# A new written order for a linear-attention and MLP block on one core: the memset behind the first statistics, thirteen warming products, keys and states regrouped

## The chip, the cores and the metric

The kernel runs on one core of one Trainium2 chip. The core has five engines that work side by side: TensorE (PE, with its weight loads as PEld) for matrix products, VectorE (DVE), ScalarE (ACT), GpSimd (POOL), and SyncE (SP), which here issues all transfers. The metric is the device time of one execution in microseconds (us), of which the median of several runs is given; a profiled execution gives the span of the trace, which is a little shorter than the device time.

## The reference

```python
def _A_ref(x, wqkv, wo):            # x: 1 x 2048 x 512, H = 32 heads of 16
    qkv = (x @ wqkv) split into q, k, v by head
    phi = lambda t: jnp.where(t > 0, t + 1, jnp.exp(t)) + 1e-6
    pq, pk = phi(q), phi(k)
    kv = jnp.einsum("bhsd,bhse->bhde", pk, v)
    z = jnp.einsum("bhsd->bhd", pk)
    num = jnp.einsum("bhqd,bhde->bhqe", pq, kv)
    den = jnp.einsum("bhqd,bhd->bhq", pq, z)[..., None] + 1e-6
    return (num / den) as 2048 x 512 @ wo

h = x + _A_ref(_layernorm(x), wqkv, wo)
h2 = h + relu(_layernorm(h) @ w1) @ w2      # w1: 512 x 1792, w2: 1792 x 512
```

All inputs and the output are bf16.

## The kernel before

The 2048 rows are 16 tiles of 128 (the first index of most steps), in four chunks of four tiles; 512 columns are four blocks of 128. The whole program is one table of words, `ORDER`. A word names a step and its indices: `K.3.7` is the key product of tile 3 into PSUM bank 7. A loop at the end of the kernel calls the steps in the table's order, with no scheduler behind it. So each engine runs its own steps exactly in the order of the words, and waits (by semaphores that are put in from the data) where an operand is not there yet. Moving a word moves instructions only against those of the same engine.

The steps that matter here:

- `lx`, `lk`, `lq`, `lv`, `lo`, `l1`, `l2` (L201, L204): loads of x, of the key, query and value parts of wqkv, of wo, w1 and w2, issued by SP. `const` (L174 to L178): four memsets on VectorE, the first of them of `zeros` (a row of `m_sb`), and the identity on POOL. `warm.n.b` (L215): n products 128x128 by 128x512 of `zeros` into bank b, whose result nobody reads.
- Layernorm of x: `S.t` statistics (L226, VectorE), `A.t` their aggregation (L227), `R.t.n` the reciprocal standard deviation of n tiles (L232 and L233, two activations on ScalarE), `N.t` the normalized tile (L251, VectorE). `T.t.b` transposes tiles 0 to 3 on TensorE (L270, four products by the identity), `E.t` copies the result out of PSUM (L280, ScalarE). Tiles 4 to 15 are transposed by DMA instead: `X.t` (L291), issued by SP.
- Keys: `K.t.b` (L299, four products of 128x512; `K.t.b.k.n` only n of them, from block k), then exp `F` (L317) and relu `U` (L320) on ScalarE, min `M` (L324) and sum `D` (L327) on VectorE, or `W` (L332) in place of `U` and `D`. The state x^T phi(k) is summed over the tiles by `G.t` (L351, four products) in banks 4 to 7. `Q` (L307) with `qF`, `qU`, `qM`, `qD`, `qW` are the same for queries. `za`, `zf`, `z` sum phi(k).
- `kv` (L392) multiplies the state by the value weights; `m` (L404) multiplies by wo; `dn` to `dm` make the denominator and scale the queries; `h` (L494) and `hD` (L500) are the attention's output plus x; `s`, `a`, `r`, `n` and `x` or `t`, `e` its layernorm and transposes.
- MLP: `p.c.f.b` (L510, four products), evacuated with relu in pairs by `pA` (L516, ScalarE) or `pD` (L521, VectorE); `f` (L530) the second product; `fo` (L538) scales and adds, `fd` (L545) stores.

There are eight PSUM banks, and the table names the bank of each product, so a product also waits until what its bank held is read.

Of the kernel before, what the change touches and what calls it, by code (L numbers as in the profile page):

```python
# [15 lines left out]


ORDER = """
const masks table lx.0.1 lx.1.1 lx.2.2 lk.0.2 lk.2.2 lx.4.2 lx.6.2 lx.8.4 lx.12.4 S.0 S.1 A.0 S.2 warm.1.6 A.1
R.0.1 S.3 A.2 R.1.1 warm.9.6 N.0 A.3 N.1 R.2.1 R.3.1 N.2 N.3 warm.1.6 T.0.2 T.1.7 T.2.5 S.4 E.0 S.5 T.3.4 A.4  # L20
K.0.3.0.2 E.1 K.1.0.0.2 E.2 E.3 A.5 R.4.2 K.0.3.2.2 S.7 F.0.1 N.5 S.6 K.3.7 M.0.1 K.2.2.0.2 U.0.1 A.7 A.6
K.1.0.2.2 D.0.1 F.3.1 U.3.1 R.6.2 N.4 K.2.2.2.2 M.3.1 G.0 D.3.1 G.3 F.2.1 F.1.1 N.6 N.7 S.8 S.9 X.5 X.4 M.2.1
A.8 A.9 U.2.1 U.1.1 K.5.1 R.8.2 K.4.0 M.1.1 D.2.1 F.4.2 D.1.1 N.9 U.4.2 N.8 X.7 S.12 X.6 X.9 G.2 K.7.3 S.13 A.12
A.13 G.1 K.6.2 K.9.1 M.4.2 S.10 R.12.2 F.6.2 N.12 D.4.2 S.11 A.10 U.6.2 X.8 lq.0.2 M.6.2 N.13 G.4 X.12 K.8.0
A.11 R.10.2 D.6.2 lv.0.2 X.13 G.5 G.6 N.10 N.11 S.15 S.14 F.8.2 M.8.2 U.8.2 G.7 X.11 A.15 A.14 D.8.2 R.14.2 N.15
K.12.0 N.14 za.2 za.4 X.10 G.9 lq.2.2 lv.2.2 K.13.1 K.11.3 F.12.2 U.12.2 X.15 X.14 l2.10.4 l2.3.4 l1.0.2 K.10.2
G.8 M.12.2 F.10.2 U.10.2 za.6 D.12.2 M.10.2 za.8 D.10.2 Q.0.0.0 Q.0.1.1 qF.0.0.2 qU.0.0.2 za.10 qM.0.0.2 K.15.3
G.12 K.14.2 F.14.2 G.11 Q.0.2.0 Q.0.3.1 qF.0.2.2 G.13 za.12 M.14.2 W.14.2 zf.12 qD.0.0.2 qM.0.2.2 qU.0.2.2 G.10
G.14 z.3.3.14 G.15 z.1.3.14 z.2.3.14 z.0.3.14 qD.0.2.2 zc Q.1.0.2 gA.0.2 gA.2.2 zh dn.0.1 Q.1.1.3 dnl.0 kv.0.4
kv.2.4 kv.1.4 kv.3.4 lo.0.2 lo.2.2 dnx.0.2.2 qF.1.0.2 dnx.0.0.2 Q.1.2.0 rt.2.7 kx qM.1.0.2 Q.1.3.1 qF.1.2.2  # L30
m.0.4 m.1.5 rv.2 qW.1.0.2 qM.1.2.2 Q.3.1.7 m.3.6 Q.2.3.2 l1.2.2 dt.3 mA.0.2 qW.1.2.2 dt.0 dt.1 m.2.5 Q.2.1.4
dn.1.3 mA.2.2 dm.0.0.2 dm.0.2.2 dnl.1 dnx.1.2.2 Q.2.2.1 h.3.6 dnx.1.0.2 h.1.5 hD.3 dt.7 qF.2.2.2 rt.6.3 s.3 dt.4
re.6 h.0.0 hD.1 qU.2.2.2 dt.5 a.3 hD.0 s.1 s.0 qM.2.2.2 a.0 Q.3.0.6 h.2.5 Q.2.0.3 n.3 n.0 a.1 dm.1.0.2 Q.3.2.0
Q.3.3.1 dm.1.2.2 x.0 x.3 hD.2 n.1 s.2 qF.3.0.2 qU.2.0.2 qF.2.0.2 h.5.2 h.6.3 a.2 qU.3.0.2 qF.3.2.2 qM.2.0.2
h.4.7 n.2 qD.2.0.2 t.2.5 qD.2.2.2 hD.5 hD.4 h.7.4 dn.2.6 hD.7 e.2 dnl.2 x.1 hD.6 qM.3.0.2 p.0.0.5 dnx.2.2.2
p.0.13.7 p.0.1.6 p.0.8.2 p.0.11.4 qD.3.0.2 s.4 dnx.2.0.2 p.0.9.3 l2.7.3 dt.10 pA.0.0.2 dt.11 l2.0.3 dt.9 dt.8
p.0.12.6 qM.3.2.2 qW.3.2.2 s.6 pD.0.12.2 p.0.3.1 p.0.2.0 pA.0.8.2 s.7 r.0.4 dn.3.6 p.0.5.3 p.0.4.2 a.7 dm.2.0.2
dnl.3 pA.0.2.2 dnx.3.0.2 dnx.3.2.2 pA.0.4.2 dm.2.2.2 p.0.7.7 h.9.0 h.8.5 p.0.6.6 n.7 s.5 dt.13 dt.12 p.0.10.3
hD.9 hD.8 s.8 a.6 pD.0.6.2 dt.15 a.4 n.6 dt.14 pA.0.10.2 f.1.1.0.7 dm.3.0.2 dm.3.2.2 h.11.0 f.1.1.7.7 h.12.4
fo.1 s.9 h.15.6 h.14.5 h.10.3 f.0.2.0.7 a.8 a.9 a.5 hD.11 n.5 hD.12 x.6 hD.15 f.3.4.0.7 h.13.7 f.3.4.7.7 x.7  # L40
s.12 n.8 n.4 hD.14 f.0.2.7.7 x.4 x.5 p.1.0.6 f.2.5.0.7 s.11 s.14 hD.13 fo.3 fo.0 hD.10 a.11 s.10 n.9 p.1.5.3
p.1.1.7 s.15 a.12 pA.1.0.2 p.1.4.2 f.2.5.7.7 p.1.13.7 p.1.3.1 a.10 n.12 r.4.4 pA.1.4.2 p.1.2.0 n.11 p.1.8.4 fo.2
a.14 a.15 s.13 p.1.12.6 n.10 p.1.7.2 pD.1.2.2 n.14 p.1.6.1 x.11 p.1.9.5 pA.1.6.2 x.10 a.13 n.15 x.9 x.8 pD.1.8.2
fd.3 f.5.3.0.7 f.7.0.0.7 p.1.10.1 fd.1 fd.0 pA.1.12.2 p.1.11.2 pA.1.10.2 p.2.9.7 p.2.11.6 f.7.0.7.7 p.2.10.5
p.2.5.1 f.5.3.7.7 fo.7 pD.2.10.2 p.2.8.6 p.2.4.0 r.8.4 f.4.4.0.7 f.4.4.7.7 fo.5 p.2.0.2 pD.2.8.2 pD.2.4.2
p.2.1.3 x.12 n.13 p.2.3.6 p.2.2.5 fd.2 f.6.0.0.7 x.14 x.13 pA.2.0.2 pA.2.2.2 x.15 fo.4 p.3.3.7 p.3.7.1 p.3.2.6
p.3.9.5 p.3.8.4 f.6.0.7.7 pD.3.2.2 fo.6 pD.3.8.2 fd.4 p.3.11.7 p.3.4.2 p.3.10.6 p.3.5.3 p.3.6.0 pA.3.10.2 fd.7
pA.3.6.2 p.2.7.7 fd.5 fd.6 p.2.6.6 pA.2.6.2 p.3.13.5 pD.3.4.2 p.3.0.1 p.3.1.2 p.2.13.7 p.2.12.6 f.11.3.0.7
p.3.12.4 pA.3.0.2 pA.2.12.2 r.12.4 pD.3.12.2 f.9.6.0.7 f.14.2.0.7 f.10.7.0.7 f.11.3.7.7 f.10.7.7.7 f.9.6.7.7
f.8.1.0.7 f.12.5.0.7 f.8.1.7.7 f.13.0.0.7 f.15.4.0.14.3.1 f.14.2.7.7 fo.9 fo.10 fo.11 fd.10 fd.11 fd.9  # L50
f.12.5.7.7 fo.8 f.13.0.7.7 f.15.3.0.14.0.2 fd.8 fo.14 fo.12 fo.13 fo.15.3.1 fd.12 f.15.1.0.14.2.1 fd.13
fd.15.3.1 fd.14 fo.15.0.2 fd.15.0.2 fo.15.2.1 fd.15.2.1
"""


# [525 lines left out]
```

## Time and profile before

| | |
|---|---|
| runs | 170.03, 170.32 and 171.63 us; median 170.32 |
| profiled execution | 170.08 us; span in the trace 168.4 us, TensorE's granted clock 0.999 in the mean |
| TensorE busy | 162.7 us, 97% of the span |
| VectorE busy | 101.2 us, 60% |
| ScalarE busy | 67.7 us, 40% |
| first warming product, first transpose, first key product | 1.25, 6.79 and 8.16 us |
| x tile 0 read by the first statistics | from 2.99 us |

Times are us from the start of the span. A row of the timeline has start, duration, engine, line, operation, written and read tiles, and in brackets the idle time ahead of it and what ended it; rows that follow each other closely are merged, with their count. A product shows 0.38 us from its start to its end but overlaps the next, so the distance of starts is what counts. The chain of work that ended last lists what each step was released by, so its pieces add up to the span.

### The profile page before, as it was taken

What the parts mean: (1) busy time and instruction counts of PE and PEld (TensorE: products, weight loads), DVE (VectorE), ACT (ScalarE), POOL (GpSimd) and SP (SyncE); (2) the same over time, 40 slices, a digit from 0 to 9 for tenths busy, and PEclk for the clock granted to TensorE, in tenths of its full rate; (3) what the DMA queues carried; (4) which work ended last, traced back from release to release, by engine and by line L of the source; (5) the groups of instructions that cost most, each with busy time, mean ns of one, the idle gap of its engine ahead of it and who ended that gap; (6) DMA issues with size and microseconds to landing.
All of it is one profiled execution on the core that took longest, in us unless ns stands there. A gap on an engine that the chain in (4) does not pass through costs nothing.

```text
span 168.4 us, 2310 instructions
## 1 busy us (share of the span) xinstructions
PE 162.7 (97%) x871; PEld 76.1 (45%) x871; DVE 101.2 (60%) x202; ACT 67.7 (40%) x100; POOL 4.8 (3%) x21
## 2 busy tenths in 40 slices
PE   7699999999999999999999999999999999999993
PEld 2244443445554454544444444444444444444552
DVE  3899998997578999786967372047203600204152
ACT  3697765847879865652000504200220245000000
POOL 7300000000000000000000000000000000000000
PEclk9999999999999999999999999999999999999999
DMA  4954566899133353535130126300320000002113
GB/s 128 339 187 94 132 123 150 231 326 351 36 64 62 75 147 72 146 62 104 27 64 0 31 42 157 82 4 0 84 72 0 31 4 0 0 0 84 40 35 93
DMA packets 30491, 15.49 MB, mean 92 GB/s; under 512 B 23184, under 2 KB 29328, under 8 KB 30480
## 3 DMA queue, kind: packets, MB, share of 16 engines
q1 hardware_dynamic: 30480, 15.34, 34.5%
q8 instruction: 7, 0.11, 0.3%
q14 instruction: 4, 0.03, 0.1%
HBM read 7.86 MB, written 2.10 MB: 59 GB/s over the span
## 4 chain that ended last, share of the span: by engine, by line
PE 94%; DMA 2%; DVE 1%; SPq 0%; issue 0%
PE bk L530 29%; PE bk L510 29%; PE bk L299 9%; PE bk L351 8%; PE bk L307 8%; PE bk L494 8%; DMA x_nat<-in_A_x_dram 2%; PE bk L270 1%; PE bk L448 1%; DVE st L226 1%; PE bk L392 1%; PE bk L404 1%; SPq L201 0%; PE bk L370 0%; DVE gT L538 0%
## 5 line engine op out<-in xcount | busy, mean ns | idle before, releaser
L530 PE MATMUL bk<-w_sb,at 128*128 128x512 bf16 (+2 forms) x252 | 50.7, 355 | 0.0
L510 PE MATMUL bk<-lnT,w_sb 128*128 128x512 bf16 x224 | 50.5, 379 | 0.0
L516 ACT ACTIVATE at<-bk 128x1024 bf16<-128x1024 f32 x17 | 17.3, 1022 | 55.6 <-PE bk L510 55.6
L530 PEld LDWEIGHTS <-at 128*128 128x128 bf16 x252 | 23.5, 98 | 25.3 <-DVE at L521 0.2
L510 PEld LDWEIGHTS <-w_sb 128*128 128x128 bf16 x224 | 21.7, 98 | 26.0
L538 DVE SCALAR_TENSOR_TENSOR gT<-bk,rstd,h_nat 128x512 bf16<-128x512 f32 (+2 forms) x18 | 12.2, 690 | 31.2 <-PE bk L530 31.2
L521 DVE TENSOR_SCALAR at<-bk 128x1024 bf16<-128x1024 f32 x11 | 13.3, 1220 | 20.7 <-PE bk L510 20.4
L317 ACT ACTIVATE eb<-bk 128x1024 bf16<-128x1024 f32 (+1 forms) x18 | 16.6, 926 | 6.9 <-PE bk L299 4.2
L307 PE MATMUL bk<-lnT,wq_sb 128*128 128x512 bf16 x64 | 15.8, 379 | 0.0
L299 PE MATMUL bk<-wk_sb,lnT 128*128 128x512 bf16 x64 | 15.5, 380 | 0.0
L494 PE MATMUL bk<-m_sb,pqs 128*128 128x512 bf16 x64 | 15.3, 379 | 0.0
L351 PE MATMUL bk<-at,h_nat 128*128 128x512 bf16 x56 | 13.7, 379 | 0.0
L320 ACT ACTIVATE rb<-bk 128x1024 bf16<-128x1024 f32 (+1 forms) x14 | 12.5, 900 | 0.7 <-PE bk L307 0.7
L500 DVE TENSOR_TENSOR h_nat<-bk,x_nat 128x512 bf16<-128x512 f32 x16 | 10.6, 681 | 2.4 <-PE bk L494 2.3
L226 DVE BATCH_NORM_STATS2 st<-x_nat 128x6 f32<-128x512 bf16 x16 | 10.5, 681 | 2.4 <-DMA x_nat<-in_A_x_dram 2.4
L228 DVE BATCH_NORM_STATS2 st<-h_nat 128x6 f32<-128x512 bf16 x16 | 10.8, 684 | 0.1
L351 PEld LDWEIGHTS <-h_nat 128*128 128x128 bf16 x64 | 6.2, 97 | 7.7 <-issue 0.7
L299 PEld LDWEIGHTS <-lnT 128*128 128x128 bf16 x64 | 5.8, 98 | 8.2 <-DMA lnT<-h_nat 1.8
L494 PEld LDWEIGHTS <-pqs 128*128 128x128 bf16 x64 | 6.2, 98 | 7.0 <-DVE pqs L484 0.3
L307 PEld LDWEIGHTS <-wq_sb 128*128 128x128 bf16 x64 | 5.9, 98 | 6.4
L461 ACT ACTIVATE wk_sb<-ld 128x1024 bf16<-128x1024 f32 x8 | 8.1, 1051 | 0.1
L324 DVE TENSOR_SCALAR eb<-eb 128x1024 bf16<-128x1024 bf16 (+1 forms) x18 | 6.9, 383 | 0.9 <-ACT eb L317 0.8
(61 smaller groups left out, 89.0 us busy)
## 6 DMA issues: line engine op xcount, KB each, us to landing
out_dram<-gT SPq DMA_DIRECT2D x15, 128.0 KB, 1.9
w_sb<-in_B_w_dram SPq DMA_DIRECT2D x2, 896.0 KB, 8.4
x_nat<-in_A_x_dram SPq DMA_DIRECT2D x2, 512.0 KB, 6.6
w_sb<-in_B_w_dram SPq DMA_DIRECT2D x2, 512.0 KB, 4.6
x_nat<-in_A_x_dram SPq DMA_DIRECT2D x3, 256.0 KB, 4.2
w_sb<-in_B_w_dram SPq DMA_DIRECT2D x2, 384.0 KB, 3.4
wk_sb<-in_A_wqkv_dram SPq DMA_DIRECT2D x2, 256.0 KB, 4.0
wq_sb<-in_A_wqkv_dram SPq DMA_DIRECT2D x2, 256.0 KB, 3.0
```

Of the source, the lines that this page charges most:

```text
L226: op_S = lambda t: nc.vector.bn_stats(out=st[:, t, :], in_=x_nat[:, t, :])
L299: nc.tensor.matmul(bk[:, b, :], lhsT=lnT[c][:, kd, j * P : (j + 1) * P], rhs=wk_sb[:, kd, :], start=(kd == 0), stop=(kd == KD - 1),)
L307: nc.tensor.matmul(bk[:, b, :], lhsT=wq_sb[:, kd, j * P : (j + 1) * P], rhs=lnT[c][:, kd, :], start=(kd == 0), stop=(kd == KD - 1),)
L317: nc.scalar.activation(out=buf(eb, kind, i, n), in_=bank(at_bank[kind, i], n), func=ACT.Exp)
L320: nc.scalar.activation(out=buf(rb, kind, i, n), in_=bank(at_bank[kind, i], n), func=ACT.Relu)
L351: nc.tensor.matmul(bk[:, KD + kd, :], lhsT=ln_nat[:, t, kd * P : (kd + 1) * P], rhs=pk(t)[:, 0, :], start=(t == 0), stop=(t == NT - 1),)
L494: nc.tensor.matmul(bk[:, b, :], lhsT=pqs[:, (c * KD + jb) % NQ, j * P : (j + 1) * P], rhs=m_sb[:, jb, :], start=(jb == 0), stop=(jb == KD ...
L510: nc.tensor.matmul(bk[:, b, cols], lhsT=w1_sb[:, kd, f * P : (f + 1) * P], rhs=lnT[c][:, kd, cols], start=(kd == 0), stop=(kd == KD - 1),)
L516: nc.scalar.activation(out=acts[c % 2][:, f : f + n, :], in_=bank(at_bank["p", c, f], n), func=ACT.Relu)
L521: nc.vector.tensor_scalar(out=acts[c % 2][:, f : f + n, :], in0=bank(at_bank["p", c, f], n), scalar1=0.0, scalar2=None, op0=ALU.max,)
L530: nc.tensor.matmul(bk[:, b, 0 : w * P], lhsT=acts[c % 2][:, f, j * P : (j + 1) * P], rhs=w2_sb[:, f, k * P : (k + w) * P], start=(f == 0), ...
L538: nc.vector.scalar_tensor_tensor(out=o_t[:, t % NO, cols], in0=bk[:, at_bank["f", t, k], 0 : w * P], scalar=rstd2[:, t : t + 1], in1=h_nat ...
```

## The change

The table of words is replaced by another one. The words are nearly the same: the three `warm` words hold eleven, one and one products where they held one, nine and one; one `qW` becomes `qU` and `qD`; twelve pairs that `pA` evacuated go to `pD` and four go the other way. No function changes. The first lines of the table:

```diff
-const masks table lx.0.1 lx.1.1 lx.2.2 lk.0.2 lk.2.2 lx.4.2 lx.6.2 lx.8.4 lx.12.4 S.0 S.1 A.0 S.2 warm.1.6 A.1
-R.0.1 S.3 A.2 R.1.1 warm.9.6 N.0 A.3 N.1 R.2.1 R.3.1 N.2 N.3 warm.1.6 T.0.2 T.1.7 T.2.5 S.4 E.0 S.5 T.3.4 A.4
+lx.0.1 lx.1.1 lx.2.2 lk.0.2 S.0 const masks lk.2.2 lx.4.2 lx.6.2 S.1 A.0 table A.1 lx.8.4 warm.11.1 lx.12.4 S.2
+S.3 A.2 A.3 R.0.1 R.1.1 N.0 N.1 T.0.0 T.1.3 R.2.1 R.3.1 N.2 warm.1.1 N.3 T.2.4 S.4 S.5 E.0 E.1 E.2 T.3.1 A.4
...
```

VectorE's first instructions (line, operation, written tile, read tiles) before and after; `m_sb` is the tile in which `zeros` lies.

```order
L576 UNCONDITIONAL_BRANCH
L174 MEMSET m_sb 128x256
L175 MEMSET eps_73 128x1
L176 MEMSET eps_74 128x1
L177 MEMSET ones 128x1
L226 BN_STATS st<-x_nat 128x6 x2
L227 BN_AGGR mv<-st 128x2
```

```order
L576 UNCONDITIONAL_BRANCH
L226 BN_STATS st<-x_nat 128x6
L174 MEMSET m_sb 128x256
L175 MEMSET eps_73 128x1
L176 MEMSET eps_74 128x1
L177 MEMSET ones 128x1
L226 BN_STATS st<-x_nat 128x6
L227 BN_AGGR mv<-st 128x2 x2
```

The statistics of tile 0 now stand ahead of the memsets. On TensorE the eleven warming products stand together ahead of T.0, as before, and two more follow: one between T.1 and T.2, one between K.3 and the rest of K.1 and K.2, whose order is K.0, half of K.2, K.3, half of K.1, then the rest (before: half of K.0, half of K.1, the rest of K.0, K.3, and the rest). Of the later keys, K.7 and K.6, K.9 and K.8, and K.15 and K.14 now stand next to each other, where a `G` stood between.

ScalarE's first steps behind the copies out of PSUM (`lnT`), as a piece of the difference: L232 and L233 are R.4 (behind `+` at its new place), L317 is F.0.

```order
 L233 ACTIVATE rstd<-rstd 128x1
 L280 ACTIVATE lnT_81<-bk 128x4x128 x4
+L317 ACTIVATE eb<-bk 128x512
+L232 ACTIVATE rstd<-mv,eps_73 128x2
+L233 ACTIVATE rstd<-rstd 128x2
+L320 ACTIVATE rb<-bk 128x512
+L317 ACTIVATE eb<-bk 128x512
+L320 ACTIVATE rb<-bk 128x512
 L232 ACTIVATE rstd<-mv,eps_73 128x2
 L233 ACTIVATE rstd<-rstd 128x2
```

F.0 now stands ahead of R.4, which N.5 and N.4 on VectorE read; before, R.4 came first.

SP's queue from the transposes of keys to the first loads of w1 (`w_sb`, 2x1792) and w2 (`w_sb`, 4x512), as a piece of the difference; `wv_sb` are the value weights that `kv` reads.

```order
-L291 DMA_TRANSPOSE lnT_84<-h_nat 128x4x128
-L204 DMA wv_sb<-in_A_wqkv_dram 128x2x512
 L291 DMA_TRANSPOSE lnT_84<-h_nat 128x4x128
 L291 DMA_TRANSPOSE lnT_83<-h_nat 128x4x128 x2
 L204 DMA wq_sb<-in_A_wqkv_dram 128x2x512
-L204 DMA wv_sb<-in_A_wqkv_dram 128x2x512
 L291 DMA_TRANSPOSE lnT_84<-h_nat 128x4x128 x2
-L204 DMA w_sb<-in_B_w_dram 128x4x512 x2
+L204 DMA w_sb<-in_B_w_dram 128x4x512
 L204 DMA w_sb<-in_B_w_dram 128x2x1792
+L204 DMA w_sb<-in_B_w_dram 128x4x512
+L204 DMA wv_sb<-in_A_wqkv_dram 128x2x512 x2
```

The two loads of the value weights moved from among the transposes to behind three loads of w2 and w1; the transpose of tile 12 (the first row shown, at its old place) moved ahead of the first load of the query weights.

More of the change, by code (lines that the diff above doesn't have):

```diff
@@ L18 @@
 ORDER = """
-const masks table lx.0.1 lx.1.1 lx.2.2 lk.0.2 lk.2.2 lx.4.2 lx.6.2 lx.8.4 lx.12.4 S.0 S.1 A.0 S.2 warm.1.6 A.1
-R.0.1 S.3 A.2 R.1.1 warm.9.6 N.0 A.3 N.1 R.2.1 R.3.1 N.2 N.3 warm.1.6 T.0.2 T.1.7 T.2.5 S.4 E.0 S.5 T.3.4 A.4
-K.0.3.0.2 E.1 K.1.0.0.2 E.2 E.3 A.5 R.4.2 K.0.3.2.2 S.7 F.0.1 N.5 S.6 K.3.7 M.0.1 K.2.2.0.2 U.0.1 A.7 A.6
-K.1.0.2.2 D.0.1 F.3.1 U.3.1 R.6.2 N.4 K.2.2.2.2 M.3.1 G.0 D.3.1 G.3 F.2.1 F.1.1 N.6 N.7 S.8 S.9 X.5 X.4 M.2.1
-A.8 A.9 U.2.1 U.1.1 K.5.1 R.8.2 K.4.0 M.1.1 D.2.1 F.4.2 D.1.1 N.9 U.4.2 N.8 X.7 S.12 X.6 X.9 G.2 K.7.3 S.13 A.12
@@ L24 @@
[L24 to L52, printed above, removed]
+lx.0.1 lx.1.1 lx.2.2 lk.0.2 S.0 const masks lk.2.2 lx.4.2 lx.6.2 S.1 A.0 table A.1 lx.8.4 warm.11.1 lx.12.4 S.2
+S.3 A.2 A.3 R.0.1 R.1.1 N.0 N.1 T.0.0 T.1.3 R.2.1 R.3.1 N.2 warm.1.1 N.3 T.2.4 S.4 S.5 E.0 E.1 E.2 T.3.1 A.4
@@ new lines @@
+K.0.6.0.2 K.0.6.2.2 E.3 F.0.1 K.2.0.0.2 A.5 R.4.2 K.3.4 warm.1.1 K.1.2.0.2 U.0.1 K.2.0.2.2 S.7 S.6 F.3.1 N.5
+U.3.1 X.5 K.1.2.2.2 A.6 N.4 A.7 M.0.1 M.3.1 R.6.2 D.0.1 F.2.1 D.3.1 U.1.1 F.1.1 U.2.1 G.0 N.7 N.6 S.8 S.9 X.4
+A.8 M.2.1 A.9 X.7 R.8.2 G.3 K.5.1 D.2.1 S.13 K.4.0 X.6 N.9 S.12 X.9 M.1.1 G.2 A.12 F.4.2 U.4.2 N.8 M.4.2 A.13
+D.1.1 S.11 K.7.3 X.8 K.6.2 R.12.2 F.6.2 N.12 N.13 G.1 K.9.1 U.6.2 X.12 D.4.2 A.11 S.10 lq.0.2 K.8.0 M.6.2 G.5
+G.4 D.6.2 A.10 G.7 G.6 S.14 F.8.2 R.10.2 X.13 N.11 M.8.2 S.15 N.10 U.8.2 D.8.2 A.15 A.14 X.11 K.12.0 G.9 K.13.1
@@ new lines @@
+X.10 za.2 R.14.2 K.11.3 N.15 F.12.2 N.14 za.4 U.12.2 lq.2.2 X.14 za.6 M.12.2 K.10.2 U.10.2 za.8 G.8 F.10.2
+Q.0.1.1 X.15 Q.0.0.0 K.15.3 M.10.2 K.14.2 qU.0.0.2 D.12.2 qF.0.0.2 G.13 Q.0.2.0 Q.0.3.1 F.14.2 D.10.2 qF.0.2.2
+za.10 za.12 M.14.2 W.14.2 zf.12 G.11 qM.0.2.2 qU.0.2.2 qM.0.0.2 qD.0.0.2 G.12 G.10 G.14 l2.10.4 z.3.1.14
+z.2.1.14 G.15 z.1.1.14 l1.0.2 l2.3.4 lv.2.2 z.0.1.14 qD.0.2.2 zc lv.0.2 Q.1.0.2 gA.0.2 gA.2.2 zh dn.0.5 Q.1.1.3
+dnl.0 kv.0.4 lo.2.2 kv.2.4 kv.1.4 kv.3.4 lo.0.2 dnx.0.2.2 qF.1.0.2 dnx.0.0.2 kx qM.1.0.2 Q.1.2.0 rt.2.7 Q.1.3.1
@@ new lines @@
+qF.1.2.2 m.0.4 m.1.5 m.3.6 rv.2 qW.1.0.2 qM.1.2.2 l1.2.2 dt.3 Q.3.1.7 Q.2.3.2 mA.0.2 qW.1.2.2 dt.0 dt.1 m.2.5
+Q.2.1.4 mA.2.2 dn.1.0 dm.0.0.2 dm.0.2.2 dnl.1 dnx.1.2.2 Q.2.2.1 h.3.6 dnx.1.0.2 h.1.3 dt.7 hD.3 qF.2.2.2 rt.6.5
+re.6 s.3 h.0.0 hD.1 qU.2.2.2 a.3 dt.4 dt.5 hD.0 s.1 s.0 qM.2.2.2 a.0 Q.3.0.6 h.2.5 Q.2.0.3 n.3 n.0 a.1 dm.1.0.2
+Q.3.2.0 Q.3.3.1 dm.1.2.2 x.3 hD.2 n.1 s.2 x.0 qF.3.0.2 qU.2.0.2 qF.2.0.2 h.5.2 h.6.3 a.2 qU.3.0.2 qF.3.2.2
+qM.2.0.2 h.4.7 n.2 qD.2.0.2 t.2.5 qD.2.2.2 qU.3.2.2 hD.5 hD.4 h.7.4 dn.2.6 hD.7 e.2 dnl.2 x.1 hD.6 qM.3.0.2
@@ new lines @@
+p.0.0.5 dnx.2.2.2 p.0.13.7 dt.10 p.0.1.6 p.0.8.2 qM.3.2.2 p.0.11.4 qD.3.0.2 s.4 dnx.2.0.2 pA.0.0.2 p.0.12.6
+p.0.9.3 p.0.3.1 dt.9 dt.8 dt.11 qD.3.2.2 s.6 p.0.2.0 r.0.4 pA.0.12.2 pD.0.8.2 s.7 pA.0.2.2 dn.3.6 dm.2.0.2 dnl.3
+p.0.5.3 p.0.4.2 a.7 dnx.3.0.2 dnx.3.2.2 dm.2.2.2 p.0.7.7 h.9.1 pD.0.4.2 l2.7.3 n.7 h.8.5 s.5 p.0.6.6 l2.0.3
+p.0.10.3 hD.9 dt.13 hD.8 dt.12 pD.0.6.2 s.8 a.6 dt.15 a.4 pD.0.10.2 n.6 f.1.1.0.7 dt.14 dm.3.0.2 dm.3.2.2 h.11.2
+f.1.1.7.7 h.12.0 fo.1 s.9 h.14.6 a.5 n.5 hD.12 h.15.4 x.6 hD.15 h.10.5 f.0.1.0.7 a.8 n.8 f.3.4.0.7 h.13.0 hD.11
@@ new lines @@
+f.3.4.7.7 a.9 x.5 s.12 n.4 hD.14 x.7 f.0.1.7.7 x.4 s.11 s.14 r.4.4 fo.3 a.11 hD.10 n.9 p.1.0.6 hD.13 fo.0
+f.2.5.0.7 p.1.5.1 s.10 s.15 a.12 x.9 p.1.1.7 f.2.5.7.7 pD.1.0.2 p.1.4.0 a.15 p.1.2.2 s.13 p.1.12.6 pD.1.4.2 fo.2
+p.1.3.3 p.1.7.1 n.11 pD.1.2.2 a.14 a.13 a.10 fd.3 p.1.13.7 p.1.8.4 pA.1.12.2 p.1.6.0 n.10 n.15 x.11 p.1.9.5 x.8
+pD.1.6.2 f.5.2.0.7 pA.1.8.2 x.10 f.7.4.0.7 p.1.10.0 fd.0 p.1.11.1 r.8.4 p.2.9.7 p.2.10.5 pD.1.10.2 f.7.4.7.7
+fo.7 p.2.5.1 p.2.11.6 n.12 pA.2.10.2 fd.1 f.4.3.0.7 n.14 p.2.8.6 n.13 f.5.2.7.7 pD.2.8.2 p.2.4.0 x.14 pD.2.4.2
@@ new lines @@
+fo.5 f.4.3.7.7 x.12 p.2.3.7 p.2.0.1 p.2.2.6 p.2.1.2 f.6.0.0.7 x.13 pA.2.0.2 x.15 p.3.7.1 fo.4 pD.2.2.2 p.3.3.6
+fd.2 p.3.2.5 p.3.9.4 p.3.8.3 pD.3.2.2 fd.5 f.6.0.7.7 fd.4 p.3.4.2 pD.3.8.2 p.3.11.5 fd.7 p.3.10.4 fo.6 p.3.5.3
+p.3.6.0 p.2.7.7 pD.3.10.2 pD.3.6.2 fd.6 p.2.6.6 pD.2.6.2 p.3.13.4 p.3.1.1 p.2.12.6 p.2.13.7 pA.3.4.2 p.3.0.0
+f.11.2.0.7 p.3.12.3 pD.3.0.2 r.12.4 pA.2.12.2 pD.3.12.2 f.9.1.0.7 f.14.6.0.7 f.10.7.0.7 f.11.2.7.7 f.9.1.7.7
+f.12.5.0.7 f.10.7.7.7 f.8.3.0.7 f.8.3.7.7 f.15.0.0.14.3.1 f.13.4.0.7 f.14.6.7.7 fo.9 fo.10 fo.11 fd.11 fd.9
@@ L53 @@
+f.12.5.7.7 fd.10 fo.8 f.13.4.7.7 f.15.2.0.14.0.2 fd.8 fo.14 fo.12 fo.13 fo.15.3.1 fd.12 fd.14 f.15.4.0.14.2.1
+fd.13 fd.15.3.1 fo.15.0.2 fd.15.0.2 fo.15.2.1 fd.15.2.1
 """
```

## The prediction

> **What bounds the kernel now.** I read the page first, then the chain of work that ended last, then the timeline of the first 14 us, then the waits.
>
> ```profile
> span 168.4 us, 2310 instructions
> PE 162.7 (97%) x871; PEld 76.1 (45%) x871; DVE 101.2 (60%) x202; ACT 67.7 (40%) x100; POOL 4.8 (3%) x21
> DVE  3899998997578999786967372047203600204152
> PE 94%; DMA 2%; DVE 1%; SPq 0%; issue 0%
> ```
>
> TensorE is 94% of the chain; VectorE (tenths of 40 slices of 4.2 us) is all but full from 4 to 34 us. The chain in order of time (start, us, what) tells where the other 6% lie, and whether TensorE's pieces run at full pace:
>
> ```profile
> 5.00 0.69 DVE st L226
> ...
> 7.93 0.40 PE bk L270 x4
> 8.32 3.45 PE bk L299 x16
> 11.78 0.92 PE bk L351 x4
> 12.70 0.04 issue
> 12.73 1.02 PE bk L351 x4
> 13.75 1.77 PE bk L299 x8
> 15.53 0.93 PE bk L351 x4
> ...
> 20.77 1.01 PE bk L299 x4
> ...
> 26.10 2.92 PE bk L299 x12
> ...
> 165.63 0.03 issue
> ```
>
> Sixteen products in 3.45 us are 0.216 us each; four are then 0.86, eight 1.73, twelve 2.59. Against that pace the rows shown lose 0.06 + 0.04 + 0.16 + 0.04 + 0.07 + 0.15 + 0.33 = 0.85 us. From the first key product (8.16 us in the timeline) to the last product at 165.63 TensorE loses nothing else worth a digit. So only three things can move the end: when the first key product starts, those 0.85 us of **old waits**, and any new wait.
>
> The start comes from this part of the timeline (start, us, engine, line, operation):
>
> ```profile
> 0.92 0.27 DVE L174 MEMSET m_sb<- 128x256 uint32 x1 [0.92 <-PEq L565]
> 1.25 3.06 PE L215 MATMUL bk<-m_sb 128*128 128x512 bf16 x7 [1.25 <-DVE ones L177]
> 2.99 1.29 DVE L226 BATCH_NORM_STATS2 st<-x_nat 128x6 f32<-128x512 bf16 x2 [1.77 <-DMA x_nat<-in_A_x_dram]
> 3.79 1.39 PE L215 MATMUL bk<-m_sb 128*128 128x512 bf16 x5
> 4.79 0.38 PE L215 MATMUL bk<-m_sb 128*128 128x512 bf16 x1
> 6.35 0.38 DVE L251 TENSOR_SCALAR h_nat<-x_nat,mv,rstd 128x512 bf16<-128x512 bf16 x1
> 6.79 1.53 PE L270 MATMUL bk<-ident,h_nat 128*128 128x128 bf16 x16 [1.61 <-DVE h_nat L251]
> 7.33 2.04 ACT L280 ACTIVATE lnT<-bk 128x512 bf16<-128x512 bf16 x4
> 8.16 3.62 PE L299 MATMUL bk<-wk_sb,lnT 128*128 128x512 bf16 x16
> ```
>
> Eleven warming products start at 1.25, 0.33 us behind the memset that they read. Seven of them are slow: the first starts at 1.25, the seventh at 3.79, so six steps of 0.42 us. Four at 0.216 follow; the last starts at 4.79, so the next slot is 5.01. TensorE then idles until the normalized tile 0 is there (6.79). The warming is free in this kernel: nothing waits for it.
>
> **The change, part by part.**
>
> *1. The memset behind the statistics of tile 0.* VectorE works in order, and the memset now stands behind S.0, which waits for its load until 2.99. The pair S.0, S.1 takes 1.29 us and a lone one 0.69 (the row at 5.00), so the next instruction starts 0.60 behind the first: the memset at 3.59, the first warming product at 3.59 + 0.33 = 3.92, in place of 1.25. Queued behind it on TensorE is everything. On VectorE the memsets fall into the wait for tile 2 (5.00), so N.0 stays at about 6.4, and tile 0 is ready for its transposes at 6.8 as before.
>
> *2. Eleven warming products ahead of T.0.* With seven of them at 0.42 they take 5.01 - 1.25 = 3.76 us: T.0 at 7.68. If none were slow, 11 x 0.216 = 2.38, the warming would end at 6.30 and T.0 start at 6.8. If all eleven were slow, T.0 starts at 7.68 + 4 x 0.21 = 8.52. The nearest row says seven, but it is one start of the kernel, and the runs shown reach from 170.03 to 171.63 us, so something at this scale varies. I take nine at 0.42, **T.0 at 8.10**, 1.31 later than before, and keep 6.8 and eleven at 0.42 with slow transposes behind them as the ends.
>
> On this step-up the Trainium skill, page "TensorE: Matmul & The Clock Gate", section "Part 1: The HAM clock gate (the "warmup" mystery)", says that the clock opens at the end of a free-running window of about 3.4 us in which TensorE was busy, whatever the kernel's start. The row agrees as far as one start can: the slow stretch of 2.9 us is shorter than such a window, so it began inside one. By that rule the next opening here would be an estimated 4.15 + 3.41 = 7.56 us, with eight or nine slow products and T.0 near 8.0, against 7.68 by the row alone.
>
> *3. From T.0 to the first key product.* E.0 starts 0.54 behind T.0 (7.33 - 6.79), takes 0.60 and steps by (2.04 - 0.60) / 3 = 0.48. With 0.1 from its end to the product, K.0 starts at T.0 + 1.24 = 9.34, **1.18 later** than 8.16. It is less than 1.31 since the later transposes no longer wait for N.1 to N.3. The warming product between T.1 and T.2 hides beside E.0, which is the later one; uncovered it would cost 0.22.
>
> *4. The key products of tiles 0 to 3 in a new order.* K.2 follows K.0 and waits for E.2, K.3 for E.3: E.2 ends at T.0 + 2.10 and E.3 at T.0 + 2.58, with the 0.1 that makes 0.10 and 0.05 of wait. The warming product behind K.3 costs a full slot, **0.22**, as the keys behind it have their data.
>
> *5. The first state product, and N.5.* These rows of ACT, DVE and SP show what it waits for.
>
> ```profile
> 9.32 0.30 ACT L232 ACTIVATE rstd<-mv,eps 128x2 f32<-128x2 f32 x1
> 9.65 0.20 ACT L233 ACTIVATE rstd<-rstd 128x2 f32<-128x2 f32 x1
> 9.76 0.58 ACT L317 ACTIVATE eb<-bk 128x512 bf16<-128x512 f32 x1
> 9.88 0.41 DVE L251 TENSOR_SCALAR h_nat<-x_nat,mv,rstd 128x512 bf16<-128x512 bf16 x1
> 20.68 0.57 SPq L204 DMA_DIRECT2D wv_sb<-in_A_wqkv_dram  x1
> 21.34 5.37 SPq L291 DMA_TRANSPOSE lnT<-h_nat  x3
> 27.95 2.50 SPq L291 DMA_TRANSPOSE lnT<-h_nat  x2
> 32.22 0.98 SPq L204 DMA_DIRECT2D wo_sb<-in_A_wo_dram  x2
> ```
>
> R.4 stood ahead of F.0 and now stands behind it. F.0 follows E.3 at T.0 + 2.48, R.4 ends 0.47 + 0.53 later, and N.5 starts at about T.0 + 3.52 = 11.6 in place of 9.88; behind it in VectorE's queue are A.6, N.4, A.7, M.0, M.3, D.0. Summing their durations, D.0 ends at T.0 + 5.1 and G.0 waits 0.10. N.5 also releases the first transpose by DMA: issued at T.0 + 3.95, landing 2.5 us later (the median row below), T.0 + 6.45, ahead of K.5's slot at T.0 + 6.9. X.4, one issue (1.25) behind, lands at T.0 + 7.7, just at K.4's slot. New waits in 4 and 5 together: **0.25**.
>
> *6. The old waits.* Two kinds: 0.37 us at G.0, G.3 and the two groups behind them, where TensorE came too early for D.0 and D.3 and for X.4, and 0.48 us for transposes by DMA at K.8 and at K.13 to K.10.
>
> ```profile
> lnT<-h_nat SPq DMA_TRANSPOSE x12, 2.5
> PEld L299 <- DMA lnT<-h_nat: 1.8, 4, 0.5
> wo_sb<-in_A_wo_dram SPq DMA_DIRECT2D x2, 256.0 KB, 7.7
> 42.61 1.06 PE L392 MATMUL bk<-gT,wv_sb 128*128 128x128 bf16 x16
> ```
>
> The three transposes at 21.34 needed 5.37 us of SP's queue, two at 27.95 only 2.50: the load of wv at 20.68 stood ahead of the three. The change takes both loads of wv from there, and TensorE arrives over a microsecond later, so I count all **0.85** as gone. Bounds: none gone and all gone. The wv loads now stand behind three loads of w2 and w1, where wo stood (32.22); wo took 7.7 us, so wv lands near 40, 2.6 us or more ahead of its product at 42.61 plus the shift. If that cover went, TensorE would stand still by what lies beyond it.
>
> *7. Evacuations.* Eight pairs more go to VectorE, fewer to ScalarE.
>
> ```profile
> L516 ACT ACTIVATE at<-bk 128x1024 bf16<-128x1024 f32 x17 | 17.3, 1022 | 55.6 <-PE bk L510 55.6
> L521 DVE TENSOR_SCALAR at<-bk 128x1024 bf16<-128x1024 f32 x11 | 13.3, 1220 | 20.7 <-PE bk L510 20.4
> ```
>
> 8 x 1.22 = 9.8 us more on VectorE, which stood waiting 20.7 us ahead of just these instructions, while a pair takes TensorE 1.73: 0, with 0.2 us per pair as the price if a bank came late. qW.3.2 becomes qU and qD; qU lies in ScalarE's gap ahead of e.2, of 0.77 us, and pushes it by the rest of its 1.02 less the 0.10 by which neighbours overlap, so by some 0.15 us:
>
> ```profile
> 60.32 0.60 ACT L286 ACTIVATE lnT<-bk 128x512 bf16<-128x512 bf16 x1 [0.77 <-PE bk L270]
> 61.38 7.93 PE L510 MATMUL bk<-lnT,w_sb 128*128 128x512 bf16 x36
> ```
>
> e.2 ended at 60.92, its reader started at 61.38, 0.46 later: 0 (0.4 if that cover were gone). All else is order inside TensorE's full stretch: 0.
>
> **The sum**: 1.18 + 0.25 + 0.22 - 0.85 = 0.80. The profiled execution took 170.08 us, span 168.4 and 1.7 around it; 170.08 + 0.80 = 170.9. It lies 0.24 under the median 170.32, and the new kernel's runs should scatter as much, so I forecast **171.1 us**, +0.5%.
>
> **The rivals.**
>
> *The clock opens late (slower).* The warming now ends on the critical path, so a late clock is paid for, where before 1.6 us of idle time hid it. If all eleven products, the sixteen transposes and the extra product are slow, T.0 starts at 8.52 and the sixteen cost another 16 x 0.06 = 1.0 and the product 0.2: K.0 at 8.52 + 1.24 + 1.2 = 10.96, 1.6 later than in my sum: 172.7. It decides when the slow stretch exceeds 4.7 us (11 x 0.42), counted from 3.92. Against it: 2.9 us in the row; for it: the run of 171.63. The Trainium skill's free-running window (same section) would place the opening anywhere within 3.4 us, so by it this case comes in some of the runs. Chance 0.17.
>
> *New waits (slower).* Keys and state products come too early for the later N.5 and its transposes: X.4, X.6 and X.8 have hardly any slack in step 5, and one missed transpose costs up to 0.5 (the longest of the four waits). If the 0.85 stays and 0.5 is added: 172.4. For: VectorE is all but full there and loses 1.1 us waiting for R.4; against: TensorE is later by the same. Chance 0.13.
>
> *The delay is absorbed (no change).* Few slow products, T.0 near 7.3, old waits gone: 170.3. Chance 0.15.
>
> *The change does what its words say and no more, at no price.* If the clock is full at the first product, T.0 stays at 6.8, G.0 comes 0.4 later, 0.85 goes: 169.9. The slow products of the row speak against it. Chance 0.05. The forecast keeps 0.50.
>
> **How the numbers follow.** The range must reach into the absorbed case below and both slower ones above: 170.2 to 172.5. One per cent (1.7 us) is about what a measurement can tell from no change. Over 172.0 lie the late clock and most of the new waits, 0.25 with a little of the forecast's own upper end taken against what of the rivals stays under it; under 168.6 nothing that I can name, since 157 us of the span are back-to-back products: 0.02. The rest, 0.73, is within 1%.
>
> **What would show it.** The first warming product near 3.9 and none idle between it and T.0; T.0 between 7.4 and 8.6; K.0 near 9.3; R.4 on ScalarE behind F.0 and N.5 near 11.6; G.0 about 1.5 later than 11.67; from K.5 to the end no wait for lnT; the wv product not waiting for a DMA. I am wrong if K.0 starts before 8.5, or if TensorE loses over 0.5 us anywhere behind 14 us.

## The result and the profile after

The changed kernel takes 172.35 us in the median of 22 runs (171.47 to 173.33), the kernel before in the same 22 rounds 170.70 (169.72 to 172.14). The ratio is **1.0087**, with a 95% interval of 1.0063 to 1.0111: a loss of 1.5 us, a little under one per cent. The forecast was +0.5% and within one per cent. Single executions of both kernels scatter by 2 us, and the profiled one of the changed kernel took 172.80 us, so its rows show a case somewhat worse than the middle.

The page of the changed kernel: the span, the busy time of the engines, and the shares of the chain that ended last.

```profile
span 171.1 us, 2293 instructions
PE 162.6 (95%) x857; PEld 76.8 (45%) x873; DVE 109.6 (64%) x210; ACT 60.3 (35%) x93; POOL 4.7 (3%) x21
PE 88%; DVE 5%; DMA 3%; ACT 2%; issue 1%
```

TensorE is as busy as before (162.6 against 162.7 us; sixteen of its product records are missing from this trace, 857 against 873 weight loads), but its share of the chain fell from 94% to 88%. The chain in order of time (start, us, what), from the first warming product to the keys of tile 8, then K.13, K.11 and K.10, and its end:

```profile
4.38 4.87 PE bk L215 x11
...
9.72 2.06 ACT lnT L280 x4
11.78 0.49 ACT eb L317
12.28 0.18 ACT rstd L232
...
12.71 0.41 DVE h_nat L251
...
15.33 1.20 DVE st L226 x2
...
19.77 3.13 DMA lnT<-h_nat
22.91 0.05 issue
22.95 1.04 PE bk L299 x4
23.99 3.24 PE bk L351 x15
...
29.17 2.59 PE bk L299 x12
...
168.38 0.35 DVE gT L538
```

Two things are new in it. Ahead of 9.7 us stand the warming products, which were on no path before. And from 9.72 to 22.95 us, 13 us in which the chain of before was made of TensorE's products alone, the chain runs over ScalarE, VectorE and one transpose by DMA. It passes F.0 (L317), R.4 (L232), N.5 (L251), then seven microseconds of VectorE's other steps, and X.8 (the DMA), and ends in the wait of K.8. From there on TensorE is dense again.

The same places in the timeline of the changed kernel:

```profile
3.36 0.69 DVE L226 BATCH_NORM_STATS2 st<-x_nat 128x6 f32<-128x512 bf16 x1 [3.36 <-DMA x_nat<-in_A_x_dram]
4.05 0.27 DVE L174 MEMSET m_sb<- 128x256 uint32 x1
4.38 4.87 PE L215 MATMUL bk<-m_sb 128*128 128x512 bf16 x11 [4.38 <-DVE ones L177]
9.05 0.92 PE L270 MATMUL bk<-ident,h_nat 128*128 128x128 bf16 x8
10.47 2.40 PE L299 MATMUL bk<-wk_sb,lnT 128*128 128x512 bf16 x10
13.16 9.15 SPq L291 DMA_TRANSPOSE lnT<-h_nat  x7
14.38 1.04 PE L351 MATMUL bk<-pk_lo,h_nat 128*128 128x512 bf16 x4
22.95 1.04 PE L299 MATMUL bk<-wk_sb,lnT 128*128 128x512 bf16 x4 [0.51 <-DMA lnT<-h_nat]
32.46 1.89 PE L307 MATMUL bk<-lnT,wq_sb 128*128 128x512 bf16 x8
```

and of the kernel before, its first query product and its last VectorE instruction:

```profile
29.73 1.89 PE L307 MATMUL bk<-lnT,wq_sb 128*128 128x512 bf16 x8
165.65 0.35 DVE L538 SCALAR_TENSOR_TENSOR gT<-bk,rstd,h_nat 128x128 bf16<-128x128 f32 x1 [0.30 <-PE bk L530]
```

Split the 2.73 us by which the last VectorE instruction starts later (168.38 against 165.65). The first key product comes 10.47 - 8.16 = **2.31** later. From it to the first query product it takes 21.99 in place of 21.57: **0.42** more. From there to the last instruction 135.92 in both: **nothing**. Everything happens ahead of the queries.

Three executions (176.75, 290.22 and 349.97 us) lie far from all others and are left out of all ratios; the longest was the profiled execution of the last experiment, so no row of that one is used.

### The profile page after: what moved, and what is told of

It is laid out like the page before. It is cut to its first block, busy times and chain, and to the rows that moved or that the text cites. A ratio compares the mean times of both kernels' runs of the same rounds, so it can differ in the third digit from the quotient of the medians.

```text
span 171.1 us, 2293 instructions
## 1 busy us (share of the span) xinstructions
PE 162.6 (95%) x857; PEld 76.8 (45%) x873; DVE 109.6 (64%) x210; ACT 60.3 (35%) x93; POOL 4.7 (3%) x21
## 4 chain that ended last, share of the span: by engine, by line
PE 88%; DVE 5%; DMA 3%; ACT 2%; issue 1%
PE bk L530 28%; PE bk L510 28%; PE bk L494 8%; PE bk L307 8%; PE bk L351 6%; PE bk L299 4%; PE bk L215 3%; DVE st L226 2%; DMA lnT<-h_nat 2%; DMA x_nat<-in_A_x_dram 1%; ACT lnT L280 1%; DVE h_nat L251 1%; PE bk L448 1%; DVE eb L324 1%; PE bk L270 1%
## 5 line engine op out<-in xcount | busy, mean ns | idle before, releaser
L521 DVE TENSOR_SCALAR at<-bk 128x1024 bf16<-128x1024 f32 x19 | 23.2, 1223 | 27.2 <-PE bk L510 25.3
L516 ACT ACTIVATE at<-bk 128x1024 bf16<-128x1024 f32 x9 | 9.2, 1023 | 55.0 <-PE bk L510 50.4
L317 ACT ACTIVATE eb<-bk 128x1024 bf16<-128x1024 f32 (+1 forms) x18 | 16.6, 930 | 5.8 <-PE bk L299 3.9
L307 PE MATMUL bk<-lnT,wq_sb 128*128 128x512 bf16 x61 | 15.1, 379 | 0.2
L320 ACT ACTIVATE rb<-bk 128x1024 bf16<-128x1024 f32 (+1 forms) x15 | 13.5, 910 | 1.2 <-PE bk L307 1.2
L351 PE MATMUL bk<-at,h_nat 128*128 128x512 bf16 x54 | 13.1, 379 | 0.1
L215 PE MATMUL bk<-m_sb 128*128 128x512 bf16 x13 | 5.6, 590 | 4.4 <-DVE ones L177 4.4
L232 ACT ACTIVATE rstd<-mv,eps 128x2 f32<-128x2 f32 (+2 forms) x14 | 4.1, 294 | 14.9 <-DVE mv L229 8.5
```

Of the source, the lines that this page charges most:

```text
L215: nc.tensor.matmul(bk[:, b, :], lhsT=zeros[:, 0:P], rhs=zeros, start=True, stop=True)
L307: nc.tensor.matmul(bk[:, b, :], lhsT=wq_sb[:, kd, j * P : (j + 1) * P], rhs=lnT[c][:, kd, :], start=(kd == 0), stop=(kd == KD - 1),)
L317: nc.scalar.activation(out=buf(eb, kind, i, n), in_=bank(at_bank[kind, i], n), func=ACT.Exp)
L320: nc.scalar.activation(out=buf(rb, kind, i, n), in_=bank(at_bank[kind, i], n), func=ACT.Relu)
L351: nc.tensor.matmul(bk[:, KD + kd, :], lhsT=ln_nat[:, t, kd * P : (kd + 1) * P], rhs=pk(t)[:, 0, :], start=(t == 0), stop=(t == NT - 1),)
L521: nc.vector.tensor_scalar(out=acts[c % 2][:, f : f + n, :], in0=bank(at_bank["p", c, f], n), scalar1=0.0, scalar2=None, op0=ALU.max,)
```

## The experiments

Each kernel differs from its parent by the words shown. All were timed in five rounds beside the kernel before, whose median was 170.42 us in every call; ratios are to that kernel, with 95% intervals. The changed kernel was timed earlier, when the kernel before had 170.70 us beside it, so a comparison with the changed kernel goes by the ratios, its own being 1.0087. In the first four kernels the table is two lines shorter, so their line numbers are two lower (L213 is L215).

**Memsets late, alone.**

```diff
 (kernel before)
-const masks table lx.0.1 lx.1.1 ... S.0 S.1
+lx.0.1 lx.1.1 ... S.0 const masks table S.1
```

> The kernel before with one edit: the memsets stand behind S.0 on VectorE. Theory START (the late memset puts the warming products on the path, the rest of the change is about neutral): first warming product at 3.9 to 4.4 us, no idle between it and T.0, T.0 at 8 to 9, first key product 1 to 2 us later than 8.2, some of it given back by the waits of before; in all +0.8 to +1.7 us. Theory REST (the later memset is hidden, the rearranged keys, R.4 and transposes cost the time): within 0.4 us of before.

Measured: 171.84 us (171.16 to 172.38), ratio 1.0070 [1.0041, 1.0098], +1.2 us. Its timeline:

```profile
4.07 4.88 PE L213 MATMUL bk<-m_sb 128*128 128x512 bf16 x11 [4.07 <-DVE ones L175]
8.73 1.60 PE L268 MATMUL bk<-ident,h_nat 128*128 128x128 bf16 x16
10.17 3.69 PE L297 MATMUL bk<-wk_sb,lnT 128*128 128x512 bf16 x16
```

The first warming product starts 4.07 in place of 1.25, the transposes follow without a gap, and the first keys come 2.0 later. One move, with the rest of the table as before, gives most of the loss. START holds for the larger part of the loss; REST as its only cause is refuted.

**Memsets first, the rest changed.**

```diff
 (changed kernel)
-lx.0.1 lx.1.1 lx.2.2 lk.0.2 S.0 const masks
+const lx.0.1 lx.1.1 lx.2.2 lk.0.2 S.0 masks
```

> The changed kernel with one edit: the memsets stand first on VectorE again. START: T.0 back at 6.8 to 7.5, the first key product near 8.2 to 8.6, and the time back to within 0.4 us of before or a little under it. REST: the time stays 1 us or more over before.

Measured: 171.39 us (170.42 to 172.37), ratio 1.0044 [1.0007, 1.0081]: neither theory's number. Taking the late memset back gives half of the loss, where adding it alone cost most of it, so the two parts do not add up. The twelve runs fall in two groups, five from 170.42 to 170.78 and seven from 171.25 to 172.37. The profiled execution, of the upper group, shows one reason. TensorE's row at T.0, and stretches of the span (from:to, length, busy us and instructions by engine, then TensorE's granted clock, DMA share, GB/s):

```profile
6.93 0.91 PE L268 MATMUL bk<-ident,h_nat 128*128 128x128 bf16 x8 [1.84 <-DVE h_nat L249]
3.90:7.30 3.40, 1.55 (x11) 0.60 (x10) 2.86 (x10) 1.64 (x8) 1.94 (x7) 1.00 0.96 319
7.30:10.70 3.40, 3.40 (x19) 2.03 (x19) 3.16 (x8) 2.26 (x5) 0.00 (x0) 0.50 0.81 315
10.70:20.00 9.30, 9.30 (x44) 3.87 (x43) 8.07 (x27) 7.66 (x19) 0.00 (x0) 1.00 0.37 72
```

The clock had opened at 3.9, TensorE then idled for 1.84 us between the last warming product and T.0, and the granted clock was 0.50 from 7.3 to 10.7 us, over most of the transposes and the first keys. So a gap in the warming is not harmless: it can close the clock again. One such stretch lowers the mean granted clock of an execution by a hundredth (it is 0.990 here), so the mean, which is on record for every run, tells where it happened: in three of the seven upper runs (0.990, the other nine runs 0.999 or 1.000). What held up the other four is not shown.

**Only the part up to the sums of keys; only the part behind them.**

```diff
 (words up to zc, then from zc)
-before, before
+changed, before        first kernel
+before, changed        second kernel
```

In both kernels the two loads of the value weights stand ahead of zc: late in the first, at their old place in the second.

> The changed kernel's words up to the sums of keys (zc), then the words of before. Both theories: all of the change's cost lies ahead of zc, so +1.2 to +1.8 us over before, like the changed kernel. If the cost lay in the evacuations by VectorE: within 0.4 us of before.

> The words of before up to zc, then those of the changed kernel, with eight pairs more evacuated by VectorE. Both theories: within 0.4 us of before. If the evacuations cost: +1 us or more.

Measured: 172.49 us (171.73 to 172.95; nine runs), 1.0096 [1.0061, 1.0131], for the changed front; 170.34 us (169.91 to 171.26), 0.9983 [0.9955, 1.0011], for the changed rest. The whole loss is ahead of zc. The eight evacuations more on VectorE and the new order of queries and MLP cost nothing that can be measured.

**R.4 ahead of F.0.**

```diff
 (changed kernel, ScalarE)
-E.3 F.0.1 ... R.4.2 U.0.1
+E.3 ... R.4.2 F.0.1 U.0.1
```

> The changed kernel with one edit: on ScalarE R.4 stands ahead of F.0 again. Theory CHAIN (behind the late start the path runs K.0, F.0, R.4, N.5, then SP's transposes one behind the other at 1.3 us, to the wait of 0.67 us at K.8): N.5 0.5 us earlier, K.8's wait 0.2 or less, 0.4 to 0.6 us under the changed kernel. Theory SLOTS (what the late memset doesn't explain is TensorE's own: the two extra warming products and the key products that wait for E.2 and E.3): within 0.2 us of the changed kernel.

Measured: 171.97 us (171.22 to 172.21), 1.0069 [1.0042, 1.0097], by the ratios 0.0018 or 0.3 us under the changed kernel, with intervals that overlap. In its timeline and its waits:

```profile
9.30 2.47 PE L299 MATMUL bk<-wk_sb,lnT 128*128 128x512 bf16 x10
10.54 0.32 ACT L232 ACTIVATE rstd<-mv,eps 128x2 f32<-128x2 f32 x1
11.12 0.41 DVE L251 TENSOR_SCALAR h_nat<-x_nat,mv,rstd 128x512 bf16<-128x512 bf16 x1 [0.65 <-ACT rstd L233]
PEld L299 <- DMA lnT<-h_nat: 0.7, 1, 0.7
```

N.5 starts 1.82 behind the first key product, against 2.24 in the changed kernel (12.71 - 10.47), and one wait of 0.7 of the weight loads for a transpose is left where there were three of 1.8 us together. K.8 starts 0.551 us behind the product ahead of it, so 0.34 of its wait of 0.67 is left, and the first query product comes 21.59 us behind the first key product in place of 21.99. That is CHAIN's direction and place; in the profiles it has the size too (0.4 us), while 0.3 us between the medians falls short of the 0.4 to 0.6 that it expected and is not clear of noise.

**Five warming products in place of eleven.**

```diff
 (changed kernel)
-warm.11.1
+warm.5.1
```

> The changed kernel with five warming products ahead of T.0 in place of eleven, the memsets still late. START (the products ahead of T.0 hold up the path): T.0 where tile 0 is ready, 1 to 2 us earlier; transposes and the first keys at half pace until the clock opens; 0.5 to 1 us under the changed kernel. If the count of slow products doesn't matter because the clock opens at the same instant and the work behind is paced by it: within 0.3 us of the changed kernel.

Measured: 172.07 us (170.80 to 172.93), 1.0085 [1.0050, 1.0121]. The profiled execution (171.09 us):

```profile
4.07 2.31 PE L215 MATMUL bk<-m_sb 128*128 128x512 bf16 x5 [4.07 <-DVE ones L177]
6.83 1.03 PE L270 MATMUL bk<-ident,h_nat 128*128 128x128 bf16 x8 [0.44 <-DVE h_nat L251]
8.85 2.32 PE L299 MATMUL bk<-wk_sb,lnT 128*128 128x512 bf16 x10
```

T.0 starts when tile 0 is ready, 1.3 us ahead of the 8.1 that I had forecast for eleven products, yet the first keys come only 0.5 ahead of my 9.34, since the transposes run at half pace. Here it wins; but four of the twelve runs lie below 171.4 and eight at 171.97 or above, and by the ratios the kernel takes what the changed one takes. START misses. So the count of products ahead of T.0 is not the loss by itself: with fewer of them the transposes meet a clock that is not open yet, here until 8.75 us by the distance of the products.

**Fifteen warming products in the kernel before.**

```diff
 (kernel before)
-warm.9.6
+warm.13.6
```

> The kernel before with fifteen warming products in place of eleven, so that the idle time ahead of T.0 shrinks from 1.6 to some 0.8 us. Theory GATE (the clock closes again in those runs in which a window of 3.4 us holds most of the idle time, as in the profile with the memset first): fewer runs near 171.5, the median 0.2 to 0.5 us under before. If the scatter of before comes from the loads of x: the same as before.

Measured: 170.21 us (169.75 to 170.80), 0.9981 [0.9954, 1.0008]. The median gains 0.2, inside the interval; the scatter tells more. None of twelve runs is above 170.80, while of the 34 runs of before beside them ten lie above 171.0, up to 172.0. GATE's mark, the missing upper runs, is there, and the mean granted clock confirms it: six of those ten have 0.988 to 0.990, while none of the twelve is below 0.999. The other four of the ten, up to 171.25, have 1.000, so the clock is not the whole scatter. The profiled execution is one in which the clock opened late, at 7.15 us by the distance of the products:

```profile
1.25 6.30 PE L215 MATMUL bk<-m_sb 128*128 128x512 bf16 x15 [1.25 <-DVE ones L177]
7.39 1.30 PE L270 MATMUL bk<-ident,h_nat 128*128 128x128 bf16 x16
```

Fifteen products took 6.3 us and delayed T.0 to 7.39, by some 0.3 us behind tile 0's readiness, and still the run took 170.21.

**Memsets first and R.4 first.**

```diff
 (changed kernel)
-lx.0.1 lx.1.1 lx.2.2 lk.0.2 S.0 const masks ... E.3 F.0.1 ... R.4.2
+const lx.0.1 lx.1.1 lx.2.2 lk.0.2 S.0 masks ... E.3 ... R.4.2 F.0.1
```

> The changed kernel with both edits: the memsets first and R.4 ahead of F.0. CHAIN and START together: within 0.3 us of before or under it. SLOTS: like the kernel with the memsets first, 0.6 us or more over before.

Measured: 170.80 us (170.37 to 172.14), 1.0026 [0.9991, 1.0061]. Again two groups: eight runs from 170.37 to 171.00, four from 172.02 to 172.14. The distance of 1.4 us is near what a clock that closed again would cost over transposes and first keys (3.4 us at half the pace is 1.7 us of work), and just these four runs have a mean granted clock of 0.990, the other eight 0.998 to 1.000. The median is 0.38 over before, between the two expectations. The wait at K.8 remains even so:

```profile
9.74 0.68 DVE st L226
10.42 0.31 DVE h_nat L251
...
17.39 3.20 DMA lnT<-h_nat
20.59 0.05 issue
20.64 1.04 PE bk L299 x4
```

With R.4 out of the way N.5 follows VectorE's statistics in the chain, and in the timeline it still starts 2.2 us behind the first key product (10.34 against 8.13).

**K.8 behind G.5.**

```diff
 (changed kernel)
-K.9.1 ... K.8.0 ... G.5 G.4
+K.9.1 ... G.5 K.8.0 G.4
```

> The changed kernel with one edit: the key product of tile 8 stands behind the state product of tile 5 again, as it stood behind one before. Theory NEW WAIT (0.67 us of the loss is K.8 waiting for X.8, which TensorE now reaches four products earlier): no wait for lnT at K.8, and 0.4 to 0.7 us under the changed kernel. If the wait only moves on to the next product: within 0.2 us of it.

Measured: 171.89 us (171.29 to 172.49; nine runs), 1.0082 [1.0056, 1.0107]; by the ratios 0.0005 under the changed kernel, which is nothing. NEW WAIT misses. The chain of this kernel (start, us, what) shows where the time went:

```profile
22.41 0.88 PE bk L299 x4
...
23.31 1.02 ACT eb L317
...
24.79 0.41 DVE h_nat L251
...
26.05 0.40 DVE h_nat L251
26.45 0.61 DVE at L327
...
27.11 1.02 PE bk L351 x4
```

K.8 no longer waits, but its exp, and behind it R.10, N.11, N.10 and a sum of keys, now end at a state product that waits 0.53 us instead. The wait moved on by four microseconds: TensorE then waits for the loop over ScalarE and VectorE, not for that transpose.

**No extra warming products.**

```diff
 (changed kernel)
-N.2 warm.1.1 N.3 ... K.3.4 warm.1.1 K.1.2.0.2
+N.2 N.3 ... K.3.4 K.1.2.0.2
```

> The changed kernel without the two extra warming products. CHAIN (TensorE waits for X.8 at K.8 anyway, so what stands ahead of it is free): K.8's wait grows by 0.2 us or so and the time stays within 0.2 us of the changed kernel. SLOTS: 0.2 to 0.45 us under it.

Measured: 172.09 us (171.61 to 172.74; six runs), 1.0088 [1.0054, 1.0122]: the changed kernel's ratio. As far as six runs tell, the two products that the change adds are free, for the reason CHAIN gives, though at another place than I had said:

```profile
13.33 1.04 PE L351 MATMUL bk<-pk_lo,h_nat 128*128 128x512 bf16 x4 [0.21 <-ACT rstd L232]
PEld L299 <- DMA lnT<-h_nat: 1.7, 3, 0.9
```

G.0 now waits 0.2 us more for its data; it starts 4.01 behind the first key product, 3.91 in the changed kernel with a product more between them.

**Fifteen products and the value weights late.**

```diff
 (kernel before)
-warm.9.6 ... lq.0.2 ... lv.0.2 ... lq.2.2 lv.2.2 ... l2.10.4 l2.3.4 l1.0.2
+warm.13.6 ... lq.0.2 ... lq.2.2 ... l2.10.4 l2.3.4 l1.0.2 lv.0.2 lv.2.2
```

> The kernel before with fifteen warming products and the two loads of the value weights behind the three loads of w2 and w1, as in the change. If those loads delayed the transposes ahead of K.13 to K.10 (0.31 us of wait in the profile of before): 0.2 to 0.3 us under the kernel with fifteen products alone, so about 169.9. If the transposes wait for something else: like it, 170.2.

Measured: 170.15 us (169.94 to 170.79), 0.9981 [0.9958, 1.0004], the same as fifteen products alone, so the expected gain is not there. In the chains of this kernel and of the one with fifteen products alone:

```profile
27.15 2.59 PE bk L299 x12
```

```profile
26.57 2.59 PE bk L299 x12
```

The twelve products of K.13, K.11 and K.10 run at full pace, where they lost 0.33 us before (26.10, 2.92 us). But they do so with the loads at their old place too, so the rows do not show that the loads of the value weights were what delayed them.

**The changed kernel with every edit at once.**

```diff
 (changed kernel)
-lx.0.1 lx.1.1 lx.2.2 lk.0.2 S.0 const masks ... warm.11.1 ... warm.1.1 ... F.0.1 ... R.4.2 ... warm.1.1 ... K.8.0 ... G.5
+const lx.0.1 lx.1.1 lx.2.2 lk.0.2 S.0 masks ... warm.15.1 ... R.4.2 F.0.1 ... G.5 K.8.0
```

> The changed kernel with the memsets first, fifteen warming products ahead of T.0, no extra ones, R.4 ahead of F.0 and K.8 behind G.5. START, GATE, CHAIN and NEW WAIT together: no run above 171, and 0.3 to 0.8 us under before. If one of them is no cause: at before's time or over it.

Measured: 170.66 us, ten runs from 170.38 to 171.06 (one above 171), 1.0007 [0.9986, 1.0028]. No loss is left that can be measured, and the upper group of runs is gone (no mean granted clock below 0.998); but it is no faster than before. The edits were made together, so the run does not say what each of them gave. The 0.3 to 0.8 us that I expected below before are not there, so one of the old waits, or what took its place, is still in it. Without a profile of an ordinary execution of this kernel that stays open. No version clearly beats the kernel before: the two with fifteen products have the lowest medians, 170.15 and 170.21, with intervals that reach over 1.

## Why the prediction was right, and where it was not

The time came out within the range and on the forecast side, twice the size of the forecast shift. That it lies within the range is owed to the range's width, which was to hold the rivals as well: the measured ratio, 1.0087, lies halfway between that of the sum (171.1 us, 1.005) and that of the rival *new waits* (172.4 us, 1.012). And one of the prediction's own signs of being wrong came up: TensorE lost over 0.5 us at one place behind 14 us. The start of the path was right, the waits behind it were not.

- *Step 1, the memset.* Right. It starts at 4.05, the first product 0.33 behind it, as worked out from the row of before; both are 0.46 later than forecast, 0.37 of it since tile 0 itself landed later (S.0 at 3.36 against 2.99) and the rest since the memset starts where the lone S.0 ends, 0.69 behind its start and not 0.60. Alone it costs 1.2 us, by the kernel with that one move.
- *Step 2, the products at 0.42 us.* The middle was near, and the end that I kept was real. Five kernels start with the same words up to T.0; their profiled executions have T.0 at 8.19, 8.24, 8.40, 9.00 and 9.05 (the changed kernel itself, all eleven at 0.42), and the first key product at 9.30, 9.32, 9.51, 10.38 and 10.47. The forecasts, 8.10 and 9.34, fit the better executions.
- *Step 3.* K.0 came 1.42 behind T.0 in place of 1.24, since the first seven of the sixteen transposes still ran at half pace.
- *Steps 4 and 5, the waits up to G.0.* 0.25 and 0.22 forecast; measured 14.38 - 10.47 = 3.91, against sixteen products of 0.216 (3.45): 0.46. Right in size. The reading of the 0.22 was wrong: taking the product away gives nothing back, as G.0 then waits for its data.
- *Step 6, the old waits: this step failed.* "I count all 0.85 as gone." From the first key to the first query product the changed kernel takes 0.42 more; forecast were 0.47 - 0.85 = -0.38. The difference, 0.80, is the term. Most waits disappeared at the named places (the twelve products of K.13 to K.10 take 2.59 us), but the chain of the changed kernel gives the time back in one wait of 0.67 at K.8 (0.888 between two starts that are 0.216 apart at full pace). With that term at nothing the same sum gives 1.18 + 0.47 - 0.06 = 1.6 us, where 0.06 is the wait of before ahead of G.0; measured are 1.5. That the two agree so well is in part luck, as the first key product scatters by over 1 us.
- Why it failed: I counted on TensorE arriving over a microsecond later, but what it awaits comes later by as much. X.8 lands 12.54 us behind the first key product in the kernel before (20.70 - 8.16) and 12.44 in the changed one (22.91 - 10.47). In the new order TensorE reaches K.8 four products, 0.86 us, earlier, and a wait of 0.15 at K.8 became one of 0.67. I had followed the transposes by DMA only to X.4 and noted for X.8 "hardly any slack". SP issues X.8 as the sixth of seven transposes back to back, 9.15 us or 1.31 each, so once N.5 and the first transpose are late nothing catches up; and N.5 starts 2.24 us behind the first key product in place of 1.72, behind F.0 and R.4. The experiments say that this is no single near miss: when K.8 is moved out of the way, a wait turns up at a later state product.
- *Step 7 and the loads of wv.* Right: the part behind zc costs nothing (0.9983), and in the changed kernel's trace kv waits for no load.
- *The rivals.* New waits was the rival nearest to the truth, with 0.13: its wait was there, at K.8, at 0.67 where I had priced 0.5 on top of the old 0.85. The late clock was there too, in the profiled execution. How often it came in other runs is not shown: the record of the granted clock reads 1.00 ahead of the first opening too, where products still start 0.427 us apart, and the mean of that very execution is 1.000.

## What to carry to other kernels

A filler that nobody waits for is free only while it ends before the path reaches its engine; when its start is moved behind a load, the filler itself becomes the path. Before counting old waits as gained because the waiting engine comes later, ask what the awaited engines wait for: if they hang on the same late start, the wait moves along. And a kernel whose runs scatter in two groups is worth a look at the clock in each group, not only at the median.
